# Four small moves around the attention turn: eviction and transposes to the turn's end ahead of P times V, the up product on ScalarE and Pool, and another order of the score matmuls

## The chip, the cores and the metric

The kernel runs on one core of one Trainium2 chip. The metric is the time of one execution on the device in microseconds: the median of the runs shown. All times of single instructions come from one profiled execution and are counted from the start of its span.

## What is computed

One transformer block on 2048 tokens of width 512, conditioned by a vector c. Layer norms are scaled and shifted by rows of `silu(c) @ w_mod`; the attention has 32 heads of 16 for the queries and a single key and value head; the feed-forward part is a bilinear GLU of width 1792 without a nonlinearity.

```python
mod = (silu(c) @ w_mod).reshape(1, 6, 1, 512)      # sa, ca, ga, sb, cb, gb
h = layernorm(x) * (1 + ca) + sa
q = heads(h @ wq)                                   # 32 heads of 16
k, v = h @ wk, h @ wv                               # one head of 16
p = softmax(q @ k.T * 16 ** -0.5)
x = x + ga * (merge(p @ v) @ wo)
h = layernorm(x) * (1 + cb) + sb
x = x + gb * (((h @ w_gate) * (h @ w_up)) @ w_down)
```

## The kernel before

**Numbers in halves.** Operands of the big products are kept as two float16 halves, and a product is three matmuls (`TERMS`, hi times hi, lo times hi, hi times lo) that add up in one PSUM bank.

**Units, key tiles, turns.** The attention loop goes over 32 units (`u`): a unit is one block of 512 tokens (`b`, four of them) by four heads. Inside a unit it goes over 16 tiles of 128 keys (`kt`). `attend(u, kt)` handles two key tiles in two turns, so there are 512 turns. A turn puts on TensorE, one after the other:

- four score matmuls ("e", `qk_exp`, L631), each followed on ScalarE by an exponential of 128 x 512 (L633) into a tile P,
- four matmuls for the row maxima of a later unit ("m", `max_half`, L581), each followed on VectorE by a maximum over 512 columns (L584); they run some 30 steps ahead of the scores,
- side matmuls ("x", `side_half`, L499): the projections and the feed-forward part, done piece by piece beside the attention,
- at its end P times V (`pv`, L642) for the key tile before: four float32 matmuls in four column groups, eight rows of the trace.

e, m and x matmuls have at most 64 rows. They use either the lower or the upper half of the array's rows (the digit 0 or 1 in the order), and two in different halves run at the same time. That is why the order of a turn is a written list: `NO_SIDE` when no side work is open, `FEW` (four x) for the query projections, `MANY` (eight x, alternating with four e and four m) for all else. In the second of the two turns the digits are flipped (`a ^ turn`).

**A bank shared by two halves.** A side group adds up matmuls of both halves of the array in one bank. When it goes from one half to the other, `Group.half` makes the next side matmul wait for an exponential: the one of the first score matmul that was put after the last side matmul (`sync["exp"]`). In MANY the last x is followed by the last e, so the first x of a turn waits for the last exponential of the turn before.

**PSUM.** There are eight banks in a queue. A score or a maximum takes the oldest and gives it back at once (`ps_mx`), so that the next user of the bank waits for its reader; `pv`, a side group and the transposed maxima (`mxt`) hold one for longer (`ps_hold`, `ps_give`).

**What else happens in a turn.** In its middle (`j == len(order) // 2`): the functions in `ends` (that is `pv_out` of the unit before: ScalarE's eviction of P times V, L648, and five DMAs), then `posts` and timers (`drain_posts`), then `late_max`. `late_max` puts the transpose of a unit's row maxima (L608) on TensorE once the maxima of that unit are complete (`max_fin`, L601, on VectorE); the copies of the result (L613, L614) and their DMAs into `sst` follow with the next `drain_posts`. At the turn's end: evictions of side groups that are complete (`g.finish()`), then `pv`, then `late_max` once more or, if it did nothing, one item of `turns` (transposes of the second layer norm's rows, L771), then `hooks`.

**Feed-forward evictions.** A gate group's eviction copies the bank to g on ScalarE (L816). An up group's eviction multiplies the bank by g on VectorE (L822), and POOL makes the two halves of the product (L823, L824). There are 14 gate and 14 up groups for each block of tokens; the block 3 is done after the attention loop.

Of the kernel before, what the change touches and what calls it, by code (L numbers as in the profile page):

```python
# [15 lines left out]
AF = mybir.ActivationFunctionType  # L16
OP = mybir.AluOpType
# [4 lines left out]
NB = 4  # L22
# [24 lines left out]

NO_SIDE = "e0 e1 m0 m1 e0 e1 m0 m1"
FEW = "e1 m0 e0 x1 m0 x1 e0 x1 m0 x1 e1 m0"
MANY = "x1 e0 x1 m0 x1 e0 x1 e0 x1 m0 x1 m0 x1 m0 x1 e0"  # L50


@with_exitstack
def adaln_mqa_glu_kernel(ctx: ExitStack, tc: tile.TileContext, x_in, wq_in, wk_in, wv_in, wo_in,
                         wg_in, wu_in, wd_in, c_in, wm_in, out):
    nc = tc.nc
# [570 lines left out]
    def qk_exp(u, kt, p, a):  # L627
        s = sst[u % 3]
        ptl[u, kt, p, a] = work.tile([128, D], F32, name="P", tag="P", bufs=8)
        t = ps_sc()  # L630
        nc.tensor.matmul(t, kst[64 * a:64 * a + 50, kt * 128:(kt + 1) * 128],  # L631
                         s[64 * a:64 * a + 50, p, :], start=True, stop=True)
        ex = nc.scalar.activation(ptl[u, kt, p, a], t, AF.Exp)  # L633
        if sync["due"]:
            sync.update(due=False, exp=ex.ins.name)

    def pv(u, kt):
        if kt == 0:
            pvb[u] = ps_hold("pv")
        for j in range(4):  # L640
            p, a = divmod(j, 2)
            nc.tensor.matmul(pvb[u][32 * j:32 * j + 32, :], vst[:, kt, :], ptl[u, kt, p, a],  # L642
                             start=(kt == 0), stop=(kt == KT - 1))
# [40 lines left out]
    ends = []  # L684
# [74 lines left out]
    turns = deque()  # L759
# [36 lines left out]
    def ffn_work(b):  # L796

        st = {}

        def op(f, which):  # L800
            def fn(i):
                k, term = divmod(i, 3)
                wl, hl = TERMS[term]
                return W["gu"[which]][:, wl, k, f * 128:(f + 1) * 128], h2s[b][:, hl, k, :]
            return fn

        def pre(f):
            def fn():
                if f == 0:
                    st["glu"] = big.tile([128, 2, FT, BT], F16, name="glu", tag="big")  # L810
            return fn

        def gate(f):
            def fn(p):
                st["g", f] = work.tile([128, BT], F32, name="g", tag="g", bufs=2)
                nc.scalar.activation(st["g", f], p, AF.Copy, scale=2.0 ** -45)  # L816
            return fn

        def up(f):
            def fn(p):  # L820
                gf = work.tile([128, BT], F32, name="gf", tag="gf", bufs=4)
                nc.vector.tensor_tensor(gf, p, st["g", f], op=OP.mult)  # L822
                nc.gpsimd.tensor_scalar(st["glu"][:, 0, f, :], gf, 1.0, 0.0, op0=OP.mult, op1=OP.add)  # L823
                nc.gpsimd.tensor_tensor(st["glu"][:, 1, f, :], gf, st["glu"][:, 0, f, :], op=OP.subtract)  # L824
            return fn

        def dn(t):
            def fn(i):
                f, term = divmod(i, 3)
                wl, hl = TERMS[term]  # L830
                return st["glu"][:, hl, f, t * 128:(t + 1) * 128], W["d"][:, wl, f, :]
            return fn

        def fin(t):
            def fn(p):
                o = x1s[b, t]
                nc.vector.scalar_tensor_tensor(o, p, sca[:, 6:7], o, op0=OP.mult, op1=OP.add)
                r0 = b * BT + t * 128
                nc.sync.dma_start(o_rows[r0:r0 + 128, :], o)
            return fn  # L840

        gu = [g for f in range(FT) for g in (Group(3 * KC, op(f, 0), gate(f), pre(f)), Group(3 * KC, op(f, 1), up(f)))]
        return gu, [Group(3 * FT, dn(t), fin(t)) for t in range(4)]
# [197 lines left out]
    def drain_posts():  # L1041
        todo = posts[:]
        posts.clear()
        if tick[0] is not None:
            tick[0] += 1
            todo += timers.pop(tick[0], [])
        for f in todo:
            f()

    def max_half(a):  # L1050
        n = mstep[a]
        mstep[a] += 1
        if n >= len(flat):
            return
        u, i, last, ops = flat[n]
        max_parts(u)
        for op in ops[a]:
            max_mm(u, a, op)
        if a == 0:
            return  # L1060
        if u + 1 < NU and i == QPRE[u > 0]:
            load_q(u + 1)
        if i == 12:
            max_parts(u + 1)
        if last:
            max_fin(u)
            (_, f, g), = max_rows(u)
            later[mstep[1] + 1] = (f, g)

    def late_max():  # L1070
        for at in [m for m in later if m <= mstep[1]]:
            f, g = later.pop(at)
            f()
            posts.append(g)
            return True
        return False
# [7 lines left out]
    def open_gate(step):  # L1084
        if not fill:
            return False
        gate = fill[0][0]
        if gate[0] == "h2":
            return gate[1] in h2done
        return gate[0] <= step  # L1090
# [39 lines left out]
    def side_half(r):  # L1130
        while True:
            if not cur:
                if not open_gate(now[0]):
                    return
                cur.append(fill.popleft()[1])
            if not cur[0].ended():
                break
            cur.clear()
        if cur[0].did[r] < cur[0].n:
            cur[0].half(r)  # L1140

    def attend(u, kt):


        now[0] = u * NSTEP + 2 * kt
        if cur and cur[0].ended():
            cur.clear()
        side = None if u + kt == 0 else cur[0] if cur else fill[0][1] if open_gate(now[0]) else None
        style = NO_SIDE if side is None else FEW if side in qs else MANY
        order = [(w[0], int(w[1])) for w in style.split()]  # L1150
        count = {}
        for turn in range(2):
            now[0] = u * NSTEP + 2 * (kt + turn)
            drain_posts()
            for j, (what, a) in enumerate(order):
                if j == len(order) // 2:
                    for f in ends:
                        f()
                    ends.clear()
                    drain_posts()  # L1160
                    late_max()
                    hooks(u, 2 * (kt + turn))
                a = a if style is NO_SIDE else a ^ turn
                if what == "m":
                    max_half(a)
                elif what == "x":
                    side_half(a)
                else:
                    k = count[a] = count.get(a, -1) + 1
                    qk_exp(u, kt + (k // 2 if style is MANY else turn), k % 2, a)  # L1170
            assert not sync["due"]
            for g in ended:
                g.finish()
            ended.clear()
            v = u * KT + kt + turn - 1
            if v >= 0:
                pv(*divmod(v, KT))
                if v % KT == KT - 1:
                    ends.append(lambda: pv_out(u - 1))
            if not late_max() and turns:  # L1180
                _, f, post = turns.popleft()
                f()
                posts.append(post)
            hooks(u, 2 * (kt + turn) + 1)

    def hooks(u, i):
        b, g = divmod(u, UB)
        step = u * NSTEP + i
        side_step(step)
        if u > 0 and g in CHANNEL and i in (4, 8, 14):  # L1190
            if i == 4:
                nrm[:] = normalise(b - (g == 0), CHANNEL[g])
            nrm[(4, 8, 14).index(i)]()
        if i == 16 and u > 0 and g == 0:
            left = list(fill)
            fill.clear()
            gu, down = ffn_work(b - 1)
            early = max(len(left) - 2, 0)
            fill.extend(left[:early])
            fill.extend(([step + 4], w) for w in wo_work(b - 1))  # L1200
            fill.extend(left[early:])
            fill.extend((["h2", b - 1], w) for w in gu + down)

    for u in range(NU):
        if u == 1:
            side.extend(dlist)
        for kt in range(0, KT, 2):
            attend(u, kt)
# [69 lines left out]
```

## Time and profile before

| What | Value |
|---|---|
| Time, median of 3 runs | 1716.25 us (1716.1 to 1716.4) |
| Span of the profiled execution | 1713.5 us |
| Median less span | 2.75 us |
| TensorE busy | 1666.1 us (97%) |
| VectorE busy | 1393.1 us (81%) |
| ScalarE busy | 1218.4 us (71%) |
| POOL busy | 505.1 us (29%) |
| Chain that ended last | PE 86%, DVE 8%, ACT 4%, issue 2%, POOL 1% |

The profiled execution's own time is its span, 1713.5 us; what the run's time has beside it lies outside of the span. Busy time on TensorE counts matmuls from their start to a modelled end; they overlap, so that a wait of some tenths of a microsecond can hide in busy time. In the chain, a share is the time in which the last work to end was waiting for, or doing, that work.

### The profile page before, as it was taken

The numbers are of one execution on the slowest core, as the hardware profiler recorded it, in microseconds if no ns is written. First come the engines' busy times: TensorE is split into PE (matmuls) and PEld (weight loads), VectorE is DVE, ScalarE is ACT, GpSimd is POOL, SyncE is SP. The second block draws the span as 40 slices with busy tenths as digits, with TensorE's granted clock in tenths as the row PEclk, the third lists the DMA queues.
The fourth block names the chain that finished last, engine by engine and source line by source line (L and its number), as shares of the span: only waits on it lengthen the run. The fifth ranks groups of instructions, "written<-read, shape, count | busy, mean of one in ns | idle before, by whom it ended". The sixth has DMA issues, their size and how long they took to land.

```text
span 1713.5 us, 33210 instructions
## 1 busy us (share of the span) xinstructions
PE 1666.1 (97%) x12671; PEld 538.8 (31%) x12671; DVE 1393.1 (81%) x2364; ACT 1218.4 (71%) x2295; POOL 505.1 (29%) x705
## 2 busy tenths in 40 slices
PE   6799999999999999999999999999999999999999
PEld 3223333222223333333333333333323333334444
DVE  7699999999999999999989999999998999604110
ACT  3668888888888777777787777777777777771010
POOL 5724445535576751110020111101011010103130
PEclk9899999999999999999999999999999999999999
DMA  5212122311222210001100000000100000001000
GB/s 201 85 49 81 60 77 72 93 37 56 82 80 60 65 41 9 16 9 29 34 8 19 13 16 9 16 9 16 31 25 22 12 20 5 8 6 45 14 1 25
DMA packets 48939, 66.64 MB, mean 39 GB/s; under 512 B 15302, under 2 KB 29450, under 8 KB 48780
## 3 DMA queue, kind: packets, MB, share of 16 engines
q1 hardware_dynamic: 47196, 64.33, 12.2%
q8 instruction: 99, 1.62, 0.4%
q14 instruction: 60, 0.49, 0.1%
q10 hardware_dynamic: 1584, 0.20, 0.1%
HBM read 51.12 MB, written 8.92 MB: 35 GB/s over the span
## 4 chain that ended last, share of the span: by engine, by line
PE 86%; DVE 8%; ACT 4%; issue 2%; POOL 1%; ACTq 0%; POOLq 0%
PE side L499 49%; PE pv L642 26%; DVE mpart L584 7%; PE sc L631 5%; PE mx L581 3%; ACT P L633 3%; PE pk L257 1%; PE mx L771 1%; PE pq L352 0%; PE mxt L608 0%; PE sc L247 0%; ACT kwb L250 0%; PE misc L871 0%; PE pv L460 0%; PE misc L292 0%
## 5 line engine op out<-in xcount | busy, mean ns | idle before, releaser
L584 DVE TENSOR_REDUCE mpart<-mx 128x1 f32<-128x512 f32 x2016 | 1267.5, 684 | 107.7 <-PE mx L581 103.1
L633 ACT ACTIVATE P<-sc 128x512 f32<-128x512 f32 x2048 | 1093.7, 599 | 269.1 <-PE sc L631 225.7
L631 PE MATMUL sc<-sst,kst 50*128 50x512 f16 x2048 | 661.4, 379 | 0.8 <-DVE mpart L584 0.6
L581 PE MATMUL mx<-kst,sst 48*128 48x512 f16 x2032 | 617.6, 378 | 8.5 <-DVE mpart L584 5.1
L642 PE MATMUL pv<-P,vst 128*32 128x512 f32 x4096 | 546.2, 605 | 1.2
L499 PE MATMUL side<-h2T,wg 64*128 64x512 f16 (+1 forms) x1152 | 278.3, 378 | 1.5 <-ACT P L633 1.5
L499 PE MATMUL side<-h2T,wu 64*128 64x512 f16 (+1 forms) x1144 | 276.2, 378 | 1.0 <-ACT P L633 1.0
L499 PE MATMUL side<-wd,glu 64*128 64x512 f16 (+1 forms) x1008 | 234.0, 378 | 2.7 <-ACT P L633 2.7
L823 POOL TENSOR_SCALAR glu<-gf 128x512 f16<-128x512 f32 x56 | 34.6, 617 | 654.2 <-DVE gf L822 573.2
L631 PEld LDWEIGHTS <-kst 50*128 50x128 f16 x2048 | 174.5, 94 | 130.8 <-issue 109.7
L581 PEld LDWEIGHTS <-sst 48*128 48x128 f16 x2048 | 182.6, 94 | 64.1 <-issue 42.1
L499 PEld LDWEIGHTS <-wg 64*128 64x128 f16 (+1 forms) x1152 | 99.5, 95 | 209.6 <-ACT P L633 99.3
L499 PEld LDWEIGHTS <-wu 64*128 64x128 f16 (+1 forms) x1144 | 99.0, 95 | 201.7 <-ACT P L633 91.3
L642 PEld LDWEIGHTS pv<-P,vst 128*32 128x32 f32 x4096 | 80.8, 108 | 215.8 <-issue 199.7
L499 PEld LDWEIGHTS <-glu 64*128 64x128 f16 (+1 forms) x1008 | 89.1, 95 | 166.3 <-ACT P L633 66.4
L822 DVE TENSOR_TENSOR gf<-side,g 128x512 f32<-128x512 f32 x56 | 38.4, 685 | 124.0 <-PE side L499 91.0
L816 ACT ACTIVATE g<-side 128x512 f32<-128x512 f32 x56 | 33.3, 595 | 96.8 <-PE side L499 96.8
L499 PE MATMUL side<-h,wq 64*128 64x512 f16 (+1 forms) x372 | 97.0, 379 | 0.0
L499 PE MATMUL side<-wo,och 64*128 64x512 f16 (+1 forms) x336 | 79.3, 378 | 0.4 <-ACT P L633 0.2
L824 POOL TENSOR_TENSOR glu<-gf,glu 128x512 f16<-128x512 f32 x56 | 65.2, 1165 | 4.7
L190 POOL TENSOR_SCALAR rv<-st 128x1 f32<-128x1 f32 (+1 forms) x20 | 4.5, 227 | 162.4 <-DVE st L735 146.7
L909 POOL TENSOR_TENSOR kwb<-kwb,wsl 128x448 f32<-128x448 f32 (+1 forms) x40 | 47.5, 1188 | 3.1
(221 smaller groups left out, 773.7 us busy)
## 6 DMA issues: line engine op xcount, KB each, us to landing
wsl<-in_B_w_gate_dram SPq DMA_DIRECT2D x32, 224.0 KB
wsl<-in_B_w_up_dram SPq DMA_DIRECT2D x32, 224.0 KB
wsl<-in_B_w_down_dram SPq DMA_DIRECT2D x28, 256.0 KB
sst<-qd SPq DMA_DIRECT2D x186, 32.0 KB
qd<-q SPq DMA_DIRECT2D x16, 256.0 KB
oc<-ev SPq DMA_DIRECT2D x128, 32.0 KB
rr<-ri SPq DMA_DIRECT2D x16, 256.0 KB
xl<-in_A_x_dram SPq DMA_DIRECT2D x16, 256.0 KB
```

The lines of the kernel that those rows point to most:

```text
L257: nc.tensor.matmul(p, wk3[:, k].rearrange("p a r -> p (a r)"), hf(b, k), start=(k == 0), stop=(k == KC - 1))
L499: return nc.tensor.matmul(self.p, left[64 * r0:64 * r1], right[64 * r0:64 * r1], start=start, stop=self.ended())
L581: nc.tensor.matmul(m, s[64 * a:64 * a + 48, p, t * 128:(t + 1) * 128], keys, start=True, stop=True)
L584: nc.vector.tensor_reduce(part, m, axis=AX.X, op=OP.max)
L631: nc.tensor.matmul(t, kst[64 * a:64 * a + 50, kt * 128:(kt + 1) * 128], s[64 * a:64 * a + 50, p, :], start=True, stop=True)
L633: ex = nc.scalar.activation(ptl[u, kt, p, a], t, AF.Exp)
L642: nc.tensor.matmul(pvb[u][32 * j:32 * j + 32, :], vst[:, kt, :], ptl[u, kt, p, a], start=(kt == 0), stop=(kt == KT - 1))
L816: nc.scalar.activation(st["g", f], p, AF.Copy, scale=2.0 ** -45)
L822: nc.vector.tensor_tensor(gf, p, st["g", f], op=OP.mult)
L823: nc.gpsimd.tensor_scalar(st["glu"][:, 0, f, :], gf, 1.0, 0.0, op0=OP.mult, op1=OP.add)
L824: nc.gpsimd.tensor_tensor(st["glu"][:, 1, f, :], gf, st["glu"][:, 0, f, :], op=OP.subtract)
L909: nc.gpsimd.tensor_tensor(acc, acc, t, op=OP.add)
```

## The change

1. `ends` (pv_out's eviction and DMAs) is run at the end of a turn, after `g.finish()` and ahead of `pv`, instead of in its middle.
2. The second `late_max` of a turn stands ahead of `pv` instead of behind it.
3. The up product: for the blocks 0 to 2 (42 of 56 groups) ScalarE copies the bank to gf, and POOL multiplies gf by g in place. Block 3 keeps VectorE's product.
4. `MANY` has its score matmuls in the slots 0, 2, 6, 7 of eight instead of 0, 2, 3, 7; the maxima stand in 1, 3, 4, 5 instead of 1, 4, 5, 6.

```diff
-MANY = "x1 e0 x1 m0 x1 e0 x1 e0 x1 m0 x1 m0 x1 m0 x1 e0"
+MANY = "x1 e0 x1 m0 x1 e0 x1 m0 x1 m0 x1 m0 x1 e0 x1 e0"
...
                 gf = work.tile([128, BT], F32, name="gf", tag="gf", bufs=4)
-                nc.vector.tensor_tensor(gf, p, st["g", f], op=OP.mult)
+                if b == NB - 1:
+                    nc.vector.tensor_tensor(gf, p, st["g", f], op=OP.mult)
+                else:
+                    nc.scalar.activation(gf, p, AF.Copy)
+                    nc.gpsimd.tensor_tensor(gf, gf, st["g", f], op=OP.mult)
...
                 if j == len(order) // 2:
-                    for f in ends:
-                        f()
-                    ends.clear()
                     drain_posts()
                     late_max()
                     hooks(u, 2 * (kt + turn))
...
             ended.clear()
+            for f in ends:
+                f()
+            ends.clear()
+            rows_turned = late_max()
             v = u * KT + kt + turn - 1
             if v >= 0:
                 pv(*divmod(v, KT))
                 if v % KT == KT - 1:
                     ends.append(lambda: pv_out(u - 1))
-            if not late_max() and turns:
+            if not rows_turned and turns:
```

## The prediction

> **What bounds the kernel now.** I read the page's shares first, then the timeline turn by turn, because a share of 97% says little about a queue of overlapping matmuls.
>
> ```profile
> PE 1666.1 (97%) x12671; PEld 538.8 (31%) x12671; DVE 1393.1 (81%) x2364; ACT 1218.4 (71%) x2295; POOL 505.1 (29%) x705
> ...
> PEclk9899999999999999999999999999999999999999
> ```
>
> TensorE is busy all the way at full clock, so a turn of the attention loop should be as long as its matmuls need. The turn with the order MANY is the one to know. The side matmuls that run in it by halves of the array (64 rows) are these:
>
> ```profile
> L499 PE MATMUL side<-h2T,wg 64*128 64x512 f16 x960 | 234.2, 377 | 1.5 <-ACT P L633 1.5
> L499 PE MATMUL side<-h2T,wu 64*128 64x512 f16 x944 | 230.3, 377 | 1.0 <-ACT P L633 1.0
> L499 PE MATMUL side<-wd,glu 64*128 64x512 f16 x672 | 160.9, 377 | 2.7 <-ACT P L633 2.7
> L499 PE MATMUL side<-wo,och 64*128 64x512 f16 x288 | 68.8, 377 | 0.4 <-ACT P L633 0.2
> ```
>
> 960 + 944 + 672 + 288 = 2864 halves, 8 to a turn: 358 MANY turns, some 1020 us of the kernel. One of them, from the timeline (start, length, engine, line):
>
> ```profile
> 1010.28 0.39 PE L631 MATMUL sc<-sst,kst 50*128 50x512 f16 x1
> 1011.59 0.37 PE L581 MATMUL mx<-kst,sst 48*128 48x512 f16 x1
> 1011.81 0.38 PE L631 MATMUL sc<-sst,kst 50*128 50x512 f16 x1
> 1012.12 1.06 PE L642 MATMUL pv<-P,vst 128*32 128x512 f32 x8
> 1013.11 0.39 PE L499 MATMUL side<-h2T,wu 64*128 64x512 f16 x1
> ...
> 1010.71 1.60 ACT L633 ACTIVATE P<-sc 128x512 f32<-128x512 f32 x3 [0.64 <-PE sc L631]
> 1012.31 0.60 ACT L633 ACTIVATE P<-sc 128x512 f32<-128x512 f32 x1
> ```
>
> The turn starts at T = 1010.28, its seventh pair of matmuls (slot 6, where "mx" stands) at T+1.31, its eighth (slot 7) at T+1.53, pv at T+1.84, the next turn at T+2.83. From pv to the next turn is 0.99. A turn of the order FEW, whose first matmul waits for no activation, has the same step:
>
> ```profile
> 198.64 1.07 PE L642 MATMUL pv<-P,vst 128*32 128x512 f32 x8
> 199.64 0.39 PE L631 MATMUL sc<-sst,kst 50*128 50x512 f16 x1
> ```
>
> 1.00 again: so 2.83 is TensorE's own time. But a second path ends close behind it. The first side matmul of a turn waits for the last exponential of the turn before (the manual dependency in `half`). That exponential starts at 1012.31 and ends at 1012.91, and the side matmul starts at 1013.11. How much of these 0.20 is slack is shown by a turn in which ScalarE is late, because pv_out's eviction stands in front of the last exponential:
>
> ```profile
> 983.18 1.07 PE L642 MATMUL pv<-P,vst 128*32 128x512 f32 x8
> 983.27 0.69 ACT L648 ACTIVATE ev<-pv,evs 128x512 f32<-128x512 f32 x1
> 983.84 0.61 ACT L633 ACTIVATE P<-sc 128x512 f32<-128x512 f32 x1
> 984.50 0.39 PE L499 MATMUL side<-h2T,wg 64*128 64x512 f16 x1 [0.25 <-ACT P L633]
> ```
>
> The exponential ends at 984.45, TensorE goes on at 984.50: the wake-up takes 0.05, and pv to the next turn took 1.32 instead of 1.00. So the plain turn has 0.15 us of slack on the path score, exponential, side matmul. This slack decides the case.
>
> The trace's times are within a span of 1713.5 us; the runs' median is 1716.25, that is 2.75 more, and I carry that offset over. 0.2% of it, 3.4 us, is about what a measurement of this kernel can tell from no change.
>
> **The order in a turn.** MANY put its four score matmuls in slots 0, 2, 3, 7; now they stand in 0, 2, 6, 7. The last exponential is still that of slot 7, but the one of slot 6 is now right ahead of it. By rows: slot 6 starts at T+1.31; an exponential starts 0.43 after its matmul (10.71 against 10.28), T+1.74; the next starts one pitch later, and the row of three that took 1.60 gives (1.60 - 0.60)/2 = 0.50, T+2.24; it ends 0.60 later, T+2.84; plus the wake-up 0.05, T+2.89. The rows' turn was 2.83, most neighbours 2.84: the excess is 0.05 a turn. Bounds: below, 0, since TensorE's own 2.83 stays, and if an exponential starts a little sooner the chain just hides. Above, 0.13: the last exponential in the rows started 0.50 after its matmul (12.31 against 11.81), not 0.43; with that lag the end is T+2.96. I take 0.05, as the 0.43 is that of an exponential that nothing holds up.
>
> The Trainium skill, ScalarE: Activation LUTs, section What ACT_TABLE_LOAD costs, says that an activation with immediate operands takes 186 ns + 0.833 ns per element and that neighbours overlap by about 93 ns. For 512 elements that is an estimated pitch of 0.52, and the sum would be some 7 us higher by it; the row's 0.50 decides.
>
> Every third MANY turn is longer, since a group ends in it and one PSUM bank less goes round:
>
> ```profile
> 1004.53 0.39 PE L631 MATMUL sc<-sst,kst 50*128 50x512 f16 x1
> 1005.18 0.69 DVE L584 TENSOR_REDUCE mpart<-mx 128x1 f32<-128x512 f32 x1 [0.28 <-PE mx L581]
> 1005.92 0.37 PE L581 MATMUL mx<-kst,sst 48*128 48x512 f16 x1
> 1006.44 1.06 PE L642 MATMUL pv<-P,vst 128*32 128x512 f32 x8
> 1007.44 0.39 PE L499 MATMUL side<-h2T,wu 64*128 64x512 f16 x1
> ```
>
> Slot 6 waits there for the bank that the turn's first maximum frees (1005.18 + 0.69 = 1005.87): it starts at T+1.39, the turn takes 2.91. In the new order the matmul in slot 6 is a score and gets the same bank: 1.39 + 0.43 + 0.50 + 0.60 + 0.05 = 2.97, again some 0.05 more. So the excess holds for all MANY turns but the 22 with a transpose, counted next: 336 x 0.05 = +17 us (0 to 45).
>
> **Maxima turned ahead of pv.** `late_max` at a turn's end now stands before pv. What it turns is made late in that turn:
>
> ```profile
> 1017.88 1.06 PE L642 MATMUL pv<-P,vst 128*32 128x512 f32 x8
> 1018.12 0.22 DVE L601 TENSOR_REDUCE mm<-mpart 128x16 f32<-128x64 f32 x1
> 1018.88 0.28 PE L608 MATMUL mxt<-ident,mm 128*16 128x128 f32 x1
> 1019.09 0.39 PE L631 MATMUL sc<-sst,kst 50*128 50x512 f16 x1
> ...
> 170.48 1.07 PE L642 MATMUL pv<-P,vst 128*32 128x512 f32 x8
> 170.75 0.22 DVE L601 TENSOR_REDUCE mm<-mpart 128x16 f32<-128x64 f32 x1
> ```
>
> mm ends at 1018.34, 0.46 after pv began. Until now pv covered that, and the transpose cost its 0.21 (18.88 to 19.09). Ahead of pv, TensorE stands still until mm is there: 0.46 + 0.05 less what mm comes sooner, since the second maximum of the turn is asked for a slot earlier (I estimate 0.1): 0.40 a time (0.3 to 0.55). Behind the waiting transpose stand pv and the whole next turn; the 0.21 is paid as before. In FEW (second pair) 170.97 - 170.48 + 0.05 = 0.54. Of the 32 transposes, 22 stand at the end of a MANY turn, 5 of a FEW turn, the rest in mid-turn or ahead of the loop, where nothing changes: 22 x 0.40 + 5 x 0.54 = +11.5 us (5 to 15). What this edit gains, ScalarE's copy of the turned maxima under pv, was off the path. The transposes of n2 (`turns`) move too, with inputs that have long been made: 0.
>
> **pv_out at the end of a turn.** Its eviction (0.69, 32 times) stood before the last exponential and cost 0.32 as shown. Now it comes behind it, in ScalarE's gap: last exponential at T+2.24, eviction at 2.74, and the next turn's first exponential isn't ready before 2.89 + 0.43 = 3.32. Nothing waits for it. Gain: 22 x 0.32 in MANY, and for the 9 in the other orders I estimate a little less, 0.25 each: 9 in all, less 2 for the third of the turns in which a group's eviction stands there too: -7 us (-9 to -3). Its five DMAs go past half a turn of SP's queue; `normalise` asks for them in the middle of the next turn but uses them two turns later (about 5.7 us): 0.
>
> **Up product.** For 42 of the 56 groups VectorE loses a product, ScalarE gains a copy, POOL a product of two SBUF operands:
>
> ```profile
> L822 DVE TENSOR_TENSOR gf<-side,g 128x512 f32<-128x512 f32 x56 | 38.4, 685 | 124.0 <-PE side L499 91.0
> L816 ACT ACTIVATE g<-side 128x512 f32<-128x512 f32 x56 | 33.3, 595 | 96.8 <-PE side L499 96.8
> L676 POOL TENSOR_TENSOR oc<-oc,rr 128x512 f32<-128x512 f32 x15 | 19.1, 1274 | 86.1 <-DMA sst<-qd 75.2 <-DMA rr<-ri 6.2 <-DMA wsl<-in_B_w_up_dram 4.7
> L824 POOL TENSOR_TENSOR glu<-gf,glu 128x512 f16<-128x512 f32 x56 | 65.2, 1165 | 4.7
> ```
>
> VectorE frees 42 x 0.685 = 29 us that no turn waited for. The copy (0.595, as g) falls behind the last exponential into the same gap as g. POOL takes 1.27 more per six turns, next to 29% busy. If the gap is gone, a copy costs up to 0.5: 42 x 0.5 = 21; I take 0 (-2 to +6).
>
> **Sum.** 17 + 11.5 - 7 + 0 = +21: 1716.25 + 21 = 1737 us.
>
> **Rivals.** (1) The chain hides: the excess is 0 and only the transposes and evictions count: 1716 + 11.5 - 7 = 1721. For it: 0.05 is less than the spread of the lags in the rows (0.43 to 0.50). Against it: both kinds of turn give it.
> (2) Faster: the chain hides and mm is done when TensorE comes to it. mm ends 0.46 after the last slot; it would have to come 0.4 sooner, which VectorE could only do if its product was what held it back (a product of 0.685 in six turns). Then -7: 1709. It decides from the point where mm ends before T+1.84.
> (3) VectorE and POOL block each other: the maxima next to POOL's new products grow. Each of 42 products, 1.27 long, would hold VectorE, which is 92% busy in these turns, up to 1.27: +53, 1790.
>
> ```profile
> 550.00:650.00 100.00, 99.64 (x831) 30.41 (x827) 92.05 (x153) 79.07 (x150) 58.67 (x60) 1.00 0.18 51
> L584 DVE TENSOR_REDUCE mpart<-mx 128x1 f32<-128x512 f32 x139 | 88.1, 685 | 7.8 <-PE mx L581 7.6
> ...
> 1200.00:1250.00 50.00, 49.75 (x409) 15.26 (x411) 46.10 (x76) 38.04 (x72) 0.26 (x2) 1.00 0.10 29
> L584 DVE TENSOR_REDUCE mpart<-mx 128x1 f32<-128x512 f32 x69 | 43.9, 684 | 3.9 <-PE mx L581 3.9
> ```
>
> Against it: with POOL busy for 58.67 of 100 us a maximum took 685 ns, with POOL idle 684.
> The Trainium skill, Perfetto Trace Analysis, section Optimizing Scalar/DVE Operations, warns that GPSIMD and VectorE share an SBUF port, so that moving work between them might not help; these two rows show no such price for the maxima.
>
> **How the numbers follow.** Forecast 0.72, (1) 0.13, (2) 0.10, (3) 0.05. Ends of the sum: 0 + 5 - 9 - 2 = -6, or 1710, and 45 + 15 - 3 + 6 = +63, or 1779; without the outer tenth on each side, 1713 to 1764. Faster by over 3.4 us: (2) and the low end, 0.12; within: most of (1)'s lower half, 0.10; slower: 0.78.
>
> **What would show it.** Right: plain MANY turns of 2.88 to 2.90 whose side matmul starts 0.05 after the last exponential's end; turns with L608 near 3.45 with an idle PE ahead of it; turns with the eviction as long as plain ones; gf's copy within pv. Wrong: plain turns still at 2.83 (no chain), or above 2.95 (a longer lag); L608 with no wait; maxima over 0.70 next to POOL.

## The result and the profile after

The changed kernel takes **1739.8 us** (1739.0 to 1739.9) against 1716.2: ratio 1.0139, 95% interval 1.0126 to 1.0153, so 23.6 us slower. The profiled execution's span is 1738.0 us against 1713.5. The forecast was 1737.

The page of the changed kernel (shares, granted clock, chain, two groups):

```profile
PE 1680.3 (97%) x12671; PEld 544.9 (31%) x12671; DVE 1354.9 (78%) x2322; ACT 1245.9 (72%) x2337; POOL 558.5 (32%) x747
...
PEclk9799999999999999999999999999999999999999
...
PE 82%; DVE 12%; ACT 3%; DMA 1%; issue 1%; POOL 0%; SPq 0%; ACTq 0%; POOLq 0%; DVEq 0%
...
L584 DVE TENSOR_REDUCE mpart<-mx 128x1 f32<-128x512 f32 x2016 | 1251.5, 682 | 160.8 <-PE mx L581 157.1
...
L826 POOL TENSOR_TENSOR gf<-gf,g 128x512 f32<-128x512 f32 x42 | 53.5, 1274 | 534.1 <-ACT gf L825 534.1
```

The shares hardly tell that anything is wrong. TensorE is still 97% busy at full clock and does the same 12671 matmuls. POOL's busy time rose by the 53.5 us of its new products; VectorE's fell by 38.2, of which the products are 28.7 (38.4 before, 9.7 after). VectorE's maxima have not become longer (682 ns). In the chain VectorE has 12% where it had 8%, but nearly all of that rise lies between 100 and 300 us, where units 0 to 4 lost 2.7 us in all, as the sums below show. The loss is only seen turn by turn. A plain MANY turn after, from the timeline:

```profile
1006.95 0.39 PE L631 MATMUL sc<-sst,kst 50*128 50x512 f16 x1
...
1008.27 0.38 PE L631 MATMUL sc<-sst,kst 50*128 50x512 f16 x1
1008.49 0.37 PE L631 MATMUL sc<-sst,kst 50*128 50x512 f16 x1
1008.70 1.08 ACT L633 ACTIVATE P<-sc 128x512 f32<-128x512 f32 x2 [0.21 <-PE sc L631]
1008.79 1.06 PE L642 MATMUL pv<-P,vst 128*32 128x512 f32 x8
1009.84 0.09 PEld L499 LDWEIGHTS <-wu 64*128 64x128 f16 x1 [0.89 <-ACT P L633]
1009.84 0.39 PE L499 MATMUL side<-h2T,wu 64*128 64x512 f16 x1
```

With T = 1006.95, slot 6 stands at T+1.32, its exponential at T+1.75, the pair of exponentials ends at 1008.70 + 1.08 = 1009.78, and the side matmul starts 0.06 later: 2.89 for the turn, where it was 2.83. Two readings mislead here. The chain gives ScalarE 3%, as before within a point, though an exponential now ends each of these turns: the matmuls of pv have a modelled end, 1008.79 + 1.06 = 1009.85, which covers the side matmul's start, so TensorE shows no idle time and the chain stays on it. And the weight load names the exponential as its releaser also in turns that TensorE sets, where its idle time is 0.84 (such a row stands at the experiment with the slots 0, 2, 5, 7): the name tells nothing, the 0.05 more does.

A turn with a transpose, after, from the timeline:

```profile
1030.32 0.39 PE L631 MATMUL sc<-sst,kst 50*128 50x512 f16 x1
...
1032.07 1.08 ACT L633 ACTIVATE P<-sc 128x512 f32<-128x512 f32 x2 [0.21 <-PE sc L631]
1032.32 0.22 DVE L601 TENSOR_REDUCE mm<-mpart 128x16 f32<-128x64 f32 x1
...
1032.65 0.09 PEld L608 LDWEIGHTS mxt<-ident,mm 128*16 128x16 f32 x1 [0.92 <-ACT P L633]
1032.68 0.27 PE L608 MATMUL mxt<-ident,mm 128*16 128x128 f32 x1 [0.45 <-ACT P L633]
1032.88 0.16 PEld L642 LDWEIGHTS pv<-P,vst 128*32 128x32 f32 x8
1032.88 1.07 PE L642 MATMUL pv<-P,vst 128*32 128x512 f32 x8
```

TensorE stands idle for 0.45 ahead of L608. The exponential that the row names can't be what it waits for: the first of the two ends 0.60 after 1032.07, at 1032.67, when the weight load has begun. What comes in time is mm, which ends at 1032.54.

Adding up turns from pv to pv, numbered from 0 in each unit by the pv that they begin with, the units 10 to 31, whose order is MANY, took 1041.0 us after and 1021.5 before, 19.5 of the 23.6. Of the units 10 to 30, the turns 11 and 12, in or behind which the transpose stands, took 136.1 (125.7 before), turns 15 and 0, around the eviction, 124.7 (127.2 before), all others 740.1 (728.6 before). Unit 31, the last one, which has no transpose, took 40.1 (40.0 before). Units 0 to 4, with FEW, took 210.4 (207.7 before), units 5 to 9 210.9 (210.7). The rest, ahead of the first pv and behind the last, is 275.7 and 273.5, of which the stretch ahead also varies by 4 us from one execution of these kernels to another.

### The profile page after: what moved, and what is told of

It reads as the page before. It is cut to its first block, busy times and chain, and to the rows that moved or that the text cites. A ratio compares the mean times of both kernels' runs of the same rounds, so it can differ in the third digit from the quotient of the medians.

```text
span 1738.0 us, 33250 instructions
## 1 busy us (share of the span) xinstructions
PE 1680.3 (97%) x12671; PEld 544.9 (31%) x12671; DVE 1354.9 (78%) x2322; ACT 1245.9 (72%) x2337; POOL 558.5 (32%) x747
## 4 chain that ended last, share of the span: by engine, by line
PE 82%; DVE 12%; ACT 3%; DMA 1%; issue 1%; POOL 0%; SPq 0%; ACTq 0%; POOLq 0%; DVEq 0%
PE side L499 47%; PE pv L642 24%; DVE mpart L584 11%; PE sc L631 4%; PE mx L581 3%; ACT P L633 2%; PE pk L257 1%; DMA wmA<-in_w_mod_dram 1%; PE mx L771 1%; PE mxt L608 0%; DMA rc<-rs 0%; PE pq L352 0%; PE sc L247 0%; SPq L656 0%; ACT kwb L250 0%
## 5 line engine op out<-in xcount | busy, mean ns | idle before, releaser
L584 DVE TENSOR_REDUCE mpart<-mx 128x1 f32<-128x512 f32 x2016 | 1251.5, 682 | 160.8 <-PE mx L581 157.1
L826 POOL TENSOR_TENSOR gf<-gf,g 128x512 f32<-128x512 f32 x42 | 53.5, 1274 | 534.1 <-ACT gf L825 534.1
L823 DVE TENSOR_TENSOR gf<-side,g 128x512 f32<-128x512 f32 x14 | 9.7, 692 | 62.9 <-PE side L499 62.9
```

The lines of the kernel that those rows point to most:

```text
L584: nc.vector.tensor_reduce(part, m, axis=AX.X, op=OP.max)
L826: nc.gpsimd.tensor_tensor(gf, gf, st["g", f], op=OP.mult)
```

## The experiments

Ratios are to the kernel before, timed beside each kernel (its medians there 1715.1 to 1716.2 us); the interval is 95%. The first four undo one part each.

**The order undone.** In the changed kernel:

```diff
-MANY = "x1 e0 x1 m0 x1 e0 x1 m0 x1 m0 x1 m0 x1 e0 x1 e0"
+MANY = "x1 e0 x1 m0 x1 e0 x1 e0 x1 m0 x1 m0 x1 m0 x1 e0"
```

> The changed kernel with MANY's old order (score matmuls in slots 0, 2, 3, 7), all else as changed. Theory (two exponentials at a turn's end make the next turn's first side matmul wait, 0.05 us in each of some 336 turns): about 15 us less than the changed kernel, 1723 to 1727; plain MANY turns back at 2.83 to 2.84, the last exponential ending 0.2 ahead of the next side matmul. Rival (the order costs nothing, the product on ScalarE and POOL or the wait of the transpose costs all): 1738 to 1741, plain turns still 2.88 or more.

Measured: 1725.3 us, 1.0053 (1.0040 to 1.0065): 14.5 less than the changed kernel. The turns of the units 10 to 30 apart from 11, 12, 15 and 0 fall from 740.1 to 728.1, the 728.6 of before. The order costs what the chain of lags gave, a little less.

**The transposes put back behind pv.**

```diff
-            rows_turned = late_max()
             v = u * KT + kt + turn - 1
...
                     ends.append(lambda: pv_out(u - 1))
+            rows_turned = late_max()
             if not rows_turned and turns:
```

> The changed kernel with the second late_max of a turn back behind pv. Theory (ahead of pv, TensorE stands until VectorE has made mm): 10 to 13 us less, 1727 to 1730; turns with L608 at about 3.1, L608 1.0 behind pv with no wait. Rival (the transpose costs its own 0.2 wherever it stands): 1738 to 1741.

Measured: 1727.0 us, 1.0061 (1.0048 to 1.0074): 12.8 less. Turns 11 and 12 of the units 10 to 30 fall from 136.1 to 127.1, 0.43 for each of the 21 transposes; units 0 to 4 from 210.4 to 208.0, 0.48 each. From its timeline:

```profile
1024.05 1.06 PE L642 MATMUL pv<-P,vst 128*32 128x512 f32 x8
1024.21 0.22 DVE L601 TENSOR_REDUCE mm<-mpart 128x16 f32<-128x64 f32 x1
...
1025.05 0.28 PE L608 MATMUL mxt<-ident,mm 128*16 128x128 f32 x1
```

The transpose stands 1.00 behind pv again, and mm, which ends at 1024.43, has been there for 0.62.

**pv_out back in mid-turn.**

```diff
                 if j == len(order) // 2:
+                    for f in ends:
+                        f()
+                    ends.clear()
                     drain_posts()
...
-            for f in ends:
-                f()
-            ends.clear()
             rows_turned = late_max()
```

> The changed kernel with pv_out back in the middle of a turn. Theory of the prediction (in the middle, the eviction pushes the last exponential; at the end it costs nothing): 7 us more, 1745 to 1749. Rival (in the new order ScalarE has a pause between the second and the third exponential, and the eviction in mid-turn falls into it, so that its place no longer matters): 1738 to 1742.

Measured: 1741.3 us, 1.0143 (1.0127 to 1.0158): only 1.5 more, less than the two kernels can be told apart by. By units it isn't nothing: 10 to 31 take 1044.4 against 1041.0, so that the eviction's place does still matter there, but units 0 to 4 take 209.7 against 210.4, and turn 3 of unit 3 is 2.59 with pv_out in mid-turn and 3.44 with it at the end. A gain in one place stands against a loss in another.

**The up product back on VectorE.**

```diff
-                if b == NB - 1:
-                    nc.vector.tensor_tensor(gf, p, st["g", f], op=OP.mult)
-                else:
-                    nc.scalar.activation(gf, p, AF.Copy)
-                    nc.gpsimd.tensor_tensor(gf, gf, st["g", f], op=OP.mult)
+                nc.vector.tensor_tensor(gf, p, st["g", f], op=OP.mult)
```

> The changed kernel with the up product back on VectorE in all blocks. Theory (both forms lie beside longer work): within 3 us of the changed kernel, 1737 to 1743. Rival (POOL's product and VectorE's maxima hold each other up, or ScalarE's copy delays exponentials): 10 us or more less, below 1730.

Measured: 1740.1 us, 1.0138 (1.0124 to 1.0151), 0.3 from the changed kernel. The product's place is worth nothing that these runs can tell, and with it the rival of VectorE and POOL blocking each other, priced at 53 us, is gone.

The four undone parts give 14.5 + 12.8 - 1.5 - 0.3 = 25.5 us where 23.6 were lost: they add up within the intervals, each about 2 us either way. Only pv_out's part did not have its size, so it was tried alone.

**The kernel before with pv_out at the end of a turn.**

```diff
                 if j == len(order) // 2:
-                    for f in ends:
-                        f()
-                    ends.clear()
...
             ended.clear()
+            for f in ends:
+                f()
+            ends.clear()
             v = u * KT + kt + turn - 1
```

> The kernel before with one edit: pv_out at the end of a turn. Theory of the prediction: 7 us less than before, 1707 to 1711, the 0.32 of the turn behind the eviction gone in every unit. Rival (by the changed kernel's own turns, where the two turns around the eviction together fell by only 0.13 a unit while the order added 0.1): 3 to 5 us less, 1711 to 1713.

Measured: 1711.6 us, 0.9979 (0.9970 to 0.9988): 3.5 less, half of what the prediction's term says. By units: 10 to 31 take 1017.7 against 1021.5, in which turns 15 and 0 of the units 10 to 30 give 4.1 (123.1 against 127.2) and turn 0 of unit 31 another 0.3. Units 0 to 4 take 0.8 more, although the first turn of unit 0, which took 3.0, 3.7 or 4.5 in these traces whatever the edit, happens to be 0.75 shorter there.

**The same with the up product on ScalarE and POOL** (the changed kernel but for order and transposes; the edit is the one above, forward).

> The kernel before with two edits: pv_out at the end of a turn, and the up product as ScalarE's copy and POOL's product. Theory (the product lies beside longer work in the old order too): the same as with pv_out alone within 2 us. Rival (in the old order ScalarE has no pause, a copy of 0.6 pushes exponentials): up to 42 x 0.2 = 8 us more than with pv_out alone.

Measured: 1710.6 us, 0.9976 (0.9966 to 0.9985): no difference from the one without it that these runs can tell.

**Slots 0, 2, 5, 7.** Is it the changed order as such, or the two scores next to each other at the end? In the changed kernel:

```diff
-MANY = "x1 e0 x1 m0 x1 e0 x1 m0 x1 m0 x1 m0 x1 e0 x1 e0"
+MANY = "x1 e0 x1 m0 x1 e0 x1 m0 x1 m0 x1 e0 x1 m0 x1 e0"
```

> The changed kernel with the score matmuls of MANY in slots 0, 2, 5, 7: no two next to each other at the end. Theory: the exponential of slot 5 starts at T+1.53, that of slot 7 at T+2.03 at the latest, ends at 2.63, so that TensorE's own 2.83 is the turn: 15 us less than the changed kernel, 1723 to 1727. Rival (what costs is that the maxima stand earlier in the turn, or the order as such): nearer to 1740.

Measured: 1724.9 us, 1.0057 (1.0043 to 1.0071), as with the old order. From its timeline:

```profile
1004.39 1.06 PE L642 MATMUL pv<-P,vst 128*32 128x512 f32 x8
1004.50 0.60 ACT L633 ACTIVATE P<-sc 128x512 f32<-128x512 f32 x1
1005.39 0.09 PEld L499 LDWEIGHTS <-wg 64*128 64x128 f16 x1 [0.84 <-ACT P L633]
1005.39 0.39 PE L499 MATMUL side<-h2T,wg 64*128 64x512 f16 x1
```

The last exponential ends at 1005.10, the side matmul starts 0.29 later: TensorE sets the turn again, 1.00 from pv to the next turn. One slot of distance, 0.22 us, is enough.

**Slots 0, 5, 6, 7.** The other way: three exponentials in a row at the end.

```diff
-MANY = "x1 e0 x1 m0 x1 e0 x1 m0 x1 m0 x1 m0 x1 e0 x1 e0"
+MANY = "x1 e0 x1 m0 x1 m0 x1 m0 x1 m0 x1 e0 x1 e0 x1 e0"
```

> The changed kernel with the score matmuls of MANY in slots 0, 5, 6, 7: three exponentials in a row at the end. Theory: the first of the three starts at T+1.53, the last at 1.53 + 2 x 0.50 = 2.53, ends at 3.13, next turn at T+3.18: 0.30 more than in the changed kernel in some 336 turns, 100 us more, 1830 to 1845. Rival (the order costs by something else than the wait for the last exponential): no such step, below 1770.

Measured: 1868.9 us, 1.0898 (1.0883 to 1.0913): 129 more than the changed kernel, above the range that was expected. The median turn, 3.20, was nearly the 3.18 of the chain. About 25 us of the rest are another wait: with three maxima ahead of mid-turn, the mid-turn `late_max` finds a unit complete and turns it there, and TensorE waits for mm in the middle of the turn. Turns 11 took 100.1 in the units 10 to 30 (75.9 after); one of them, from the timeline:

```profile
1095.06 0.22 DVE L601 TENSOR_REDUCE mm<-mpart 128x16 f32<-128x64 f32 x1
1095.33 0.09 PEld L608 LDWEIGHTS mxt<-ident,mm 128*16 128x16 f32 x1 [1.73 <-DVE mm L601]
1095.33 0.28 PE L608 MATMUL mxt<-ident,mm 128*16 128x128 f32 x1 [1.23 <-DVE mm L601]
```

**What takes pv_out's gain: the row sums?** In every second unit `pv_out` is followed by `normalise`, which loads the row sums that pv_out's last DMA has stored. In the changed kernel, the eviction, SP's queue and VectorE's reciprocal behind unit 3 (within unit 4), from the timeline:

```profile
267.25 0.71 ACT L648 ACTIVATE ev<-pv,evs 128x512 f32<-128x512 f32 x1
267.99 2.46 SPq L656 DMA_DIRECT2D oc<-ev  x4
270.49 0.55 SPq L657 DMA_DIRECT2D rs<-ev  x1
271.14 0.39 SPq L904 DMA_DIRECT2D wsl<-in_B_w_up_dram  x1
272.23 0.33 SPq L664 DMA_DIRECT2D rc<-rs  x1
...
275.36 0.35 DVE L667 RECIPROCAL rc<-rc 128x32 f32<-128x32 f32 x1 [1.14 <-DMA rc<-rs]
```

And in the kernel before:

```profile
263.23 0.69 ACT L648 ACTIVATE ev<-pv,evs 128x512 f32<-128x512 f32 x1
263.95 2.46 SPq L656 DMA_DIRECT2D oc<-ev  x4
...
268.20 0.33 SPq L664 DMA_DIRECT2D rc<-rs  x1
...
271.55 0.35 DVE L667 RECIPROCAL rc<-rc 128x32 f32<-128x32 f32 x1 [0.17 <-DMA rc<-rs]
```

From the eviction's start to the load's issue it takes 5 us in both, but the reciprocal, which is put in a turn counted from the unit's start, does not move with it. VectorE waits for it, the maxima behind it in VectorE's queue come late, then the banks that they free, and the turn is longer: turn 3 of unit 4 took 3.83 after and 2.86 before, of unit 3 3.44 and 2.59, of unit 8 2.91 and 2.37. Three kernels had the row sums' DMA ahead of the four of oc: the changed kernel, the one with pv_out alone at the end, and that with the up product.

```diff
+        nc.sync.dma_start(rsum[b, g // 2][h:h + 4, :], ev[16:128:32, :])
         for j in range(4):
             r = 16 * (h + j)
             nc.sync.dma_start(oc[b, g // 2][r:r + 16, :], ev[32 * j:32 * j + 16, :])
-        nc.sync.dma_start(rsum[b, g // 2][h:h + 4, :], ev[16:128:32, :])
```

> The changed kernel with one more edit: in pv_out the DMA of the row sums is issued ahead of the four DMAs of the heads instead of behind them. Theory (SP issues five DMAs for 3 us, the sums last; with pv_out at the turn's end they reach the reciprocal of normalise too late, and VectorE stands): the waits of the reciprocal within the attention loop go to 0, 2 to 3 us less than the changed kernel, 1736 to 1738. Rival (the longer turns in the units 3, 4 and 8 have another cause): 1739 to 1741, turns 3.3 and 4.3 still over 3.4.

Measured: 1737.7 us, 1.0135 (1.0120 to 1.0151); 2 us less is within the interval. Turn 3 of unit 8 is mended (2.37), those of units 3 and 4 are not (3.47, 3.67).

> The kernel before with pv_out at the end of a turn and the row sums' DMA first; the up product on VectorE. Theory: the wait of the reciprocal is gone, 2 to 3 us less than with pv_out at the end alone (ratio 0.9979), ratio 0.996 to 0.9968. Rival: as with pv_out alone.

Measured: 1711.9 us, 0.9984 (0.9975 to 0.9993), no gain over 0.9979; the turns 3 of units 3 and 4 still take 3.46 and 3.25.

> The kernel before with pv_out at the end of a turn, the row sums' DMA first and the up product as ScalarE's copy and POOL's product: the version that should beat both kernels. Theory: 2 to 3 us less than without the DMA's move (ratio 0.9976), ratio 0.9958 to 0.9966, some 1709. Rival: as without it.

Measured: 1711.3 us, 0.9978 (0.9969 to 0.9986), no gain over 0.9976. The theory in this form fell: which of the five DMAs goes first isn't what makes the load late. The load itself stands behind all five and, in unit 4, a weight slice in SP's queue; with the sums first it was issued there 4.5 us behind the eviction's start, only 0.5 sooner.

**The reciprocal two steps later.** If the reciprocal is only asked for too early, moving it must do what the order of the DMAs didn't. In the kernel with pv_out at the end and the up product on ScalarE and POOL, in both places where the list of steps stands:

```diff
-(4, 8, 14)
+(4, 10, 14)
```

> The kernel before with pv_out at the end of a turn, the up product as ScalarE's copy and POOL's product, and the reciprocal of normalise one turn later (step 10 instead of 8 of a unit). Theory (what is late is the load of the sums, which stands in SP's queue behind five DMAs of pv_out and weight slices, so that the order among the five didn't matter; a later reciprocal finds it landed): the reciprocal waits for nothing in the loop, the turns 3.3 and 4.3 are near 2.5 to 2.9, 2 us less than without this edit (ratio 0.9976), ratio 0.996 to 0.997. Rival (these turns are long for another reason, or the DMA of the reciprocals becomes late for POOL's product): no less than 0.9972.

Measured: 1709.2 us, 0.9960 (0.9946 to 0.9973), the fastest here, 7 us below the kernel before. Units 0 to 4 take 206.8 us against 209.8 without this step; 1.1 of these 3.0 lie in the first two turns of unit 0, which this step doesn't touch. The turns 3 of units 3 and 4 are at 2.50, where they took 3.38 and 3.66 without it, and 2.59 and 2.86 in the kernel before. The waits of the reciprocal in the kernel before, the changed one, the one with pv_out alone at the end, and this one (sum, times, longest):

```profile
DVE rc L667 <- DMA rc<-rs: 0.2, 1, 0.2
```

```profile
DVE rc L667 <- DMA rc<-rs: 61.5, 4, 59.1
```

```profile
DVE rc L667 <- DMA rc<-rs: 2.9, 3, 1.6
```

```profile
DVE rc L667 <- DMA rc<-rs: 58.1, 1, 58.1
```

The long one of 58 to 59 us is VectorE with nothing else to do behind the loop, where the tail didn't get longer (176.5 after, 176.0 before). Within the loop it waited 61.5 - 59.1 = 2.4 us in three places after, and not at all here. The times of these last two kernels against each other, 0.9976 and 0.9960, have overlapping intervals; that the step mended these turns is shown by the waits and the turns, not by the times.

## Why the prediction was right, and where not

**Order: right.** Predicted 17 us, measured 14.5. The turn came out as worked out: slot 6 at T+1.32 for T+1.31, its exponential 0.43 behind it, 1.08 for two where 0.50 + 0.60 was taken, wake-up 0.06 for 0.05. Counted from one turn's first side matmul to the next one's, as the prediction counts, 157 of the 252 other turns of the units 10 to 30 took 2.89, and 61, in which a group ends, 2.97, both as forecast; with the old order back, 158 took 2.84 and 56 took 2.91 or 2.93. Counted from pv to pv, a turn in which a group ends shows 2.99 and the one behind it 2.87, because its pv itself comes later. The old order gave back 12.0 in these 252 turns, 0.048 each, 1.6 in the 42 turns 15 and 0, 0.04 each, and nothing in turns 11 and 12 (136.5 against 136.1), of which those behind a transpose are among the forecast's 336. That is where the forecast is too high. The bound of 0.13 did not come. The estimate by the Trainium skill, ScalarE: Activation LUTs, section What ACT_TABLE_LOAD costs, was 7 us more, from a pitch of 0.52; the two exponentials of these turns have 1.08 - 0.60 = 0.48, and most pairs in the changed kernel's trace 0.48 or 0.49, so here the measured overlap is 0.10 to 0.12 and not the page's 0.093, and the measurement decides.

**Transposes: right.** Predicted 11.5, measured 12.8; by units 0.43 each with MANY (predicted 0.40) and 0.48 with FEW (predicted 0.54). The turn itself is longer than forecast: from first side matmul to first side matmul 3.56 in 12 and 3.48 in 7 of the units 10 to 30, for 3.45. In the turn shown the weight load starts 0.11 behind mm, not 0.05, and the matmul 0.03 behind that. The turn behind it is an ordinary one again (2.89 or 2.97 in 17 of 21). mm came 0.08 sooner (T+2.22 for T+2.30); 0.1 was estimated.

**pv_out: right in direction, twice too large.** Predicted -7, measured -3.5 alone and -1.5 within the change. The part of MANY was nearly right: 22 x 0.32 less 2 is 5, and turns 15 and 0 gave 4.4 with that of unit 31. The 2 taken off stood for the wrong thing, though. In 7 of the units 10 to 30 the long turn is turn 15 and isn't the eviction's doing. From the timeline of the kernel before:

```profile
1073.02 1.07 PE L642 MATMUL pv<-P,vst 128*32 128x512 f32 x8
...
1074.45 1.60 ACT L633 ACTIVATE P<-sc 128x512 f32<-128x512 f32 x3 [0.64 <-PE sc L631]
1075.94 0.69 ACT L648 ACTIVATE ev<-pv,evs 128x512 f32<-128x512 f32 x1
1076.10 0.16 PEld L642 LDWEIGHTS pv<-P,vst 128*32 128x32 f32 x8 [0.59 <-ACT P L633]
```

and of that with pv_out alone at the end:

```profile
1071.81 1.06 PE L642 MATMUL pv<-P,vst 128*32 128x512 f32 x8
...
1074.89 0.16 PEld L642 LDWEIGHTS pv<-P,vst 128*32 128x32 f32 x8 [0.59 <-ACT P L633]
1074.89 1.06 PE L642 MATMUL pv<-P,vst 128*32 128x512 f32 x8
```

The first pv of a new unit waits for the turn's third exponential (ended at 1076.05), whose P is for the next key tile, so that what pv can need of it is the bank: 3.08 in both. Behind these seven, turn 0 lost only 0.07 (2.91 to 2.84), behind most others 0.31 or 0.32 (3.15 to 2.84, 3.26 to 2.94). The step that failed is the last of that part, "`normalise` asks for them in the middle of the next turn but uses them two turns later (about 5.7 us): 0", and with it the 9 x 0.25 for the other orders. With FEW, turns 0 did lose 0.24 each (2.74 to 2.50 in units 1 and 4), 1.1 in all around the evictions of the units 1 to 9, where 2.25 was taken. But the late reciprocal takes 0.5 to 1.0 back in the turns 3 of units 3, 4 and 8: the term put at 0 is 2.4 us in the changed kernel and 2.9 in the one with pv_out alone at the end. The five DMAs take 3 us of SP's queue, the load of the sums is issued 5.0 to 5.7 us behind the eviction's start, and the two turns that the prediction counted as 5.7 us are 4.7 to 5.0 there, where a turn takes 2.37 or 2.50. In the units 10 to 30 of the changed kernel, with their longer turns, the reciprocal never waited. A later reciprocal cured it. That this accounts for all of the difference between -3.5 and -1.5 isn't shown; both lie in each other's interval.

**Up product: right**, 0 for 0. Its copy lies within pv or behind it, and the turn behind such a copy is not longer.

**Rivals.** That the chain hides (1721 and 1709) fell with the rows of the plain turn; mm did not come in time; VectorE and POOL don't block each other, as the maxima's 682 ns beside 53.5 us more of POOL's products show.

**The sum.** That 1737 came within 3 us of 1739.8 is in part luck: order was forecast 2.5 too high, transposes 1.3 too low and pv_out 5.5 too low, so that errors of opposite sign stand against each other.

## What to carry to other kernels

An engine that is 97% busy can have another engine's path 0.15 us behind it, and reordering work "within" its turn is paid once that slack is used; read the slack from a turn in which the other engine is known to be late. When a step is moved later, go through everything that was timed against its old place: a consumer written down at a fixed step doesn't move with it, and on a queue in order its wait is paid by all that stands behind it. Of the four parts of this change two lost, one gained and one did nothing that could be told: without the two that lose, and with the consumer moved too, it is 0.4% faster instead of 1.4% slower.

## What was not expected of the hardware

Two waits cost more than one. In TensorE's queue of weight loads an extra semaphore instruction of 51 ns stands before some transposes. From the view of line L608 in the changed kernel:

```profile
L608 PE MATMUL mxt<-ident,mm x32: 268/270/380, 87.5 to 1509.7; 128*16 128x128 f32 x32
L608 PEldq EVENT_SEMAPHORE  x22: 51/51/51, 130.6 to 1462.2; - x22
```

In 22 of the 32 the weight load starts 0.11 to 0.12 after mm's end, and these are the 22 with such an instruction just ahead, which starts 0.04 after mm's end; in the other 10 it is 0.05. So a wake-up read from a consumer with one wait is 0.06 to 0.07 short for one with two. In the same way the issue of a DMA is no small thing on SP: the four of 16 rows took 2.46 us in the queue, over 0.6 each.
